# Two neighbouring PSUM banks for each tile of h, where any two were taken before, in a kernel of FFT, mixing, inverse FFT and a SoLU block

## The chip, the cores and the metric

The kernel runs on one core of a Trainium2 chip. The metric is the device time of one execution in microseconds (us); the figure of a kernel is the median of its runs. A change of under 0.5% can't be told from none here.

## The reference

```python
def _attn_ref(x, w_r, w_i, b_r, b_i):            # x: 8 x 3136 x 256
    X = np.fft.rfft(x, axis=1)
    Yr = X.real @ w_r - X.imag @ w_i + b_r
    Yi = X.real @ w_i + X.imag @ w_r + b_i
    Yr = np.sign(Yr) * np.maximum(np.abs(Yr) - 0.01, 0.0)      # Yi likewise
    return np.fft.irfft(Yr + 1j * Yi, n=3136, axis=1)

def _moe_ref(x, w_in, w_out, g_ln):              # x: 25088 tokens x 256
    h = x @ w_in                                 # 1024 wide
    e = np.exp(h - h.max(-1, keepdims=True))
    solu = h * e / (e.sum(-1, keepdims=True) + 1e-9)
    ln = (solu - solu.mean(-1)) / np.sqrt(solu.var(-1) + 1e-6) * g_ln
    return ln @ w_out
```

The output of the first function, seen as 25088 rows, is the input of the second. All data is f32 at the edges; inside, most products are made of f16 halves (a high and a low part).

## The kernel before

The FFT of length 3136 is done as 98 x 32 for each of eight batches b. In the names of the code: `fwd1` is the transform over 98 (its result goes to DRAM as `s1`), `fwd2` the one over 32 (`bin` in, `Xh` and `Xl` out), `mix` the product with w_r and w_i with the threshold (`yt`, `yc`, `y`, then `yh` and `yl`), `inv1` and `inv2` the way back (`zout` to DRAM as `s2`, `zt` in, `ring_hi` and `ring_lo` out). The ring holds the transformed rows with the 256 channels on the partitions, ready to be the stationary operand.

The second function takes tiles of 128 tokens, 196 in all. `moe_head` makes h = 128 x 1024 in PSUM: 12 matmuls of 512 columns (`win_hi`, `win_lo`, `win_low`), six for each half of h. h fills two banks, since a bank holds 512 f32 per partition. Three large instructions then read the whole of h: VectorE takes the maximum (`TENSOR_REDUCE sm<-banks`), ScalarE the exponential (`ACTIVATE u<-banks,sm,hsb`), VectorE the product (`SCALAR_TENSOR_TENSOR u<-banks,sm,u`). They are called the readers of h below. `moe_turn` splits u into halves (`lh` on ScalarE, `ll` on GpSimd) and transposes both by DMA into `th` and `tl`. `moe_tail` is the product with w_out: 16 matmuls with `th` and then 8 with `tl`, which go on adding up in the same half of one bank, that of the tile `po`; ScalarE reads it into `o` at the end.

All eight PSUM banks are one tensor, `banks` (class `Banks`). Four kinds of tiles live in it: `pf` and `pb` (the FFT of later batches and of batch 0), `ph` (h, two banks) and `po` (the tail), each with a limit on how many may be open (`BANKS`). Which bank a tile gets is decided by `Plan.order`.

`Plan` records all operations of the kernel, and `Plan.order` lists them: with estimated lengths it goes through the time of the five engines, and on each engine takes, among the operations that may start within `PATIENCE` ns of the first, the one with the lowest key. `KEYS` holds the numbers from which these keys are made: each h, tail, step of the FFT or piece of weight preparation gets a due place on the scale of token tiles. A bank is free in the plan when the last user of its tile is done. `issue` then gives the operations to the engines in the plan's order, and semaphores are set between instructions by a layer below, from the tensors and the parts of them that the instructions name. For h the named part is the slice that `Banks.place` returns:

```python
a, z = min(banks), max(banks)
return self.whole[:, a] if a == z else self.whole[:, a : z + 1 : z - a]
```

A pair of banks 3 and 6 is so a slice from 3 to 6 with step 3.

Of the kernel before, what the change touches and what calls it, by code (L numbers as in the profile page):

```python
# [39 lines left out]


KEYS = dict(
    front_b0=(-134.43, 2.81),
    w_in=(-129.4, -109.93, -44.57),
    w_out=(-102.26, -0.89),
    mix_w=30.03,
    front_a1=(-80.28, -2.98),
    front_a=((-15.77, 8.71), (-6.29, 0.76)),
    front_b=((-1.1, -4.17), (-1.83, 0.4)),
    inv2=-69.22,  # L50
    turn=2.98,
    tail=4.41,
)
BANKS = dict(pf=7, ph=8, po=8, pb=4)


def fft_constants():
# [78 lines left out]
class View:  # L136
# [5 lines left out]
    def __init__(self, tile, rows, cells, dtype, path=()):  # L142
        self.tile, self.rows, self.cells, self.dtype, self.path = tile, rows, cells, dtype, path
# [113 lines left out]
class Banks:  # L257


    def __init__(self, pool, n, **most):  # L260
        self.pool, self.kinds = pool, {name: Kind(m, self) for name, m in most.items()}
        self.n, self.whole, self.ordered = n, None, False
        self.free = [(0.0, i) for i in range(n)]

    def place(self, banks):
        if self.whole is None:
            self.whole = self.pool.tile([128, self.n, 512], F32, name="banks")
        a, z = min(banks), max(banks)
        return self.whole[:, a] if a == z else self.whole[:, a : z + 1 : z - a]

    def tile(self, name):
        t = Tile(self.pool, self.kinds[name], [128, 512], F32, dict(name=name, bufs=1))
# [8 lines left out]
class Slots:  # L281


    def __init__(self, pool, n, name, shape):
        self.pool, self.n, self.name, self.shape, self.ordered = pool, n, name, shape, True
        self.kind, self.whole = Kind(n, self), None
        self.free = [(0.0, i) for i in range(n)]

    def memory(self):
        if self.whole is None:  # L290
# [24 lines left out]
class Plan:  # L315
# [2 lines left out]


    ENGINES = ("gpsimd", "tensor", "vector", "scalar", "sync")  # L320
    PATIENCE = 150.0
    BACKLOG, AHEAD = 3200.0, 1500.0
    LEAVE = {2: 115.0, 4: 150.0, 8: 195.0}

# [102 lines left out]
    def order(self):  # L427
        ready = {e: [] for e in self.ENGINES}
        free = dict.fromkeys(self.ENGINES, 0.0)
        waits, bus, half, port = {}, 0.0, False, 0.0  # L430
        for op in self.ops:
            waits[op] = len(op.needs)
            for o in op.needs:
                o.next.append(op)
            if not op.needs:
                op.at = 0.0
                ready[op.engine].append(op)
        left = {t: len(t.users) for op in self.ops for t in op.tiles}

        turn, turns = {}, {}  # L440
        for t, op in sorted(((t, min(t.users, key=lambda op: op.seq)) for t in left), key=lambda x: (x[1].key, x[1].seq)):
            if t.kind.banks is None or t.kind.banks.ordered:
                turn[t] = turns.get(t.kind, 0)
                turns[t.kind] = turn[t] + 1
        done = []

        def may_start(op):
            at = max(free[op.engine], op.at, port if op.port else 0.0, bus - (self.AHEAD if op.early else self.BACKLOG) if op.moved else 0.0)
            taken = {}
            for t in op.tiles:  # L450
                if t.owner is None:
                    k = t.kind
                    n = len(k.placed) + taken.get(k, 0)
                    taken[k] = taken.get(k, 0) + 1
                    if turn.get(t, n) != n:
                        return np.inf
                    n -= k.bufs
                    if n >= 0:
                        at = max(at, k.freed[n] if n < len(k.freed) else np.inf)
                    if k.banks is not None:  # L460
                        n, spare = taken.get(k.banks, 0) + t.size, k.banks.free
                        taken[k.banks] = n
                        at = max(at, spare[n - 1][0] if n <= len(spare) else np.inf)
            return at

        while len(done) < len(self.ops):
            best = None
            for e in self.ENGINES:
                can = [(may_start(op), op) for op in ready[e]]
                if not can:  # L470
                    continue
                first = min(at for at, _ in can)
                if first == np.inf:
                    continue
                _, _, at, op = min((op.key, op.seq, at, op) for at, op in can if at <= first + self.PATIENCE)
                if best is None or at < best[0]:
                    best = at, op
            assert best is not None, "the plan is stuck"
            at, op = best
            e = op.engine  # L480
            ready[e].remove(op)
            if e == "tensor":
                if op.half != half:
                    at += 95.0 if op.half else self.LEAVE[half]
                half = op.half
            op.start = at
            op.end = free[e] = at + op.length
            if op.port:
                port = op.end
            if op.moved:  # L490
                bus = max(bus, op.end) + op.moved
                op.end = bus + 2000.0
            for t in op.tiles:
                if t.owner is None:
                    t.owner = op
                    t.kind.placed.append(t)
                    if t.kind.banks is not None:
                        t.banks = [t.kind.banks.free.pop(0)[1] for _ in range(t.size)]
                left[t] -= 1
                if not left[t]:  # L500
                    freed = max(o.end + self.SEEN[o.engine] for o in t.users)
                    insort(t.kind.freed, freed)
                    if t.kind.banks is not None:
                        for bank in t.banks:
                            insort(t.kind.banks.free, (freed, bank))
            for o in op.next:
                waits[o] -= 1
                if not waits[o]:
                    o.at = max(p.end + (0.0 if p.engine == o.engine == "tensor" else self.SEEN[p.engine]) for p in o.needs)
                    ready[o.engine].append(o)  # L510
            done.append(op)
        self.span = max(op.end for op in done)
        return sorted(done, key=lambda op: (op.start, op.seq))
# [22 lines left out]
def fft_mix_solu_kernel(ctx: ExitStack, tc, x, w_r, w_i, b_r, b_i, w_in, w_out, g_ln, fa, ff, iaf, fb, fs, gb, gs, ia, out):  # L536
# [17 lines left out]
    sp = Pool(ctx.enter_context(tc.tile_pool(name="sp", bufs=4)), 4)  # L554
    banks = Banks(ctx.enter_context(tc.tile_pool(name="ps", bufs=1, space=PSUM)), 8, **BANKS)

# [916 lines left out]
```

## Time and profile before

| | |
|---|---|
| median of 3 runs | 1878.6 us (1873.95 to 1882.69) |
| the profiled execution | 1879.95 us, of it 1878.2 us from the first to the last instruction (the span) |
| TensorE (PE) | 1568.8 us busy, 84% of the span |
| VectorE (DVE), ScalarE (ACT), GpSimd (POOL) | 1221.5, 1146.5 and 1173.5 us busy: 65%, 61% and 62% |
| mean granted clock of TensorE | 0.964 of the full 2.4 GHz |

PE is a busy matmul unit, PEld its weight loads. Since a helper of the kernel records every operation, all rows have one line (L425), and groups are told apart by the names of the tiles. "Idle before" a group is the time in which its engine stood idle just ahead of one of its instructions, with what ended that wait.

### The profile page before, as it was taken

The page shows a single profiled execution, that of the slowest core. Times are in us where ns is not written, and L with a number is a line of the kernel's source. Part 1 is how long each engine was busy: PE and PEld are TensorE (multiplying, and loading weights), DVE is VectorE, ACT ScalarE, POOL GpSimd, SP SyncE. Part 2 cuts the span into 40 slices and gives each one's busy share as a digit, 9 for nine tenths or more (in the row PEclk, how much of TensorE's full clock was granted, in tenths as well). Part 3 has the DMA queues.
Part 4 walks back from the last instruction along what each step waited for, and adds up shares of the span by engine and source line. Part 5 has one row for each costly group of instructions (what it writes and reads, how often), then busy time and mean ns, then how long its engine had stood idle before and what let it go on. Part 6 is the DMA issues. An engine that isn't in the chain of part 4 may idle for free. (4 is left out here: it accounts for less than half of the span.)

```text
span 1878.2 us, 41461 instructions
## 1 busy us (share of the span) xinstructions
PE 1568.8 (84%) x15471; PEld 1059.3 (56%) x15471; DVE 1221.5 (65%) x2496; ACT 1146.5 (61%) x2092; POOL 1173.5 (62%) x1701
## 2 busy tenths in 40 slices
PE   6977988878887888988986879887788888778888
PEld 3444665646555565665654556565555666455555
DVE  4996777556765676867774567666677666545543
ACT  4776766565656565666664567565566666456665
POOL 1646876656755676677664667666676666555565
PEclk7989999989999999999998999999999999999999
DMA  6895878546787766988676767777665955456655
GB/s 212 246 263 120 181 176 169 138 99 142 159 172 158 139 146 146 202 181 169 142 172 139 150 135 163 165 175 161 139 136 129 191 100 116 88 112 124 124 101 107
DMA packets 538815, 285.69 MB, mean 152 GB/s; under 512 B 428900, under 2 KB 507216, under 8 KB 538612
## 3 DMA queue, kind: packets, MB, share of 16 engines
q1 hardware_dynamic: 538164, 281.43, 68.7%
q8 instruction: 121, 1.98, 0.5%
q10 hardware_dynamic: 448, 1.61, 0.3%
q14 instruction: 82, 0.67, 0.1%
HBM read 103.10 MB, written 77.07 MB: 96 GB/s over the span
## 5 line engine op out<-in xcount | busy, mean ns | idle before, releaser
L425 POOL TENSOR_TENSOR ll<-u,lh 128x1024 f16<-128x1024 f32 x196 | 420.2, 2144 | 191.5 <-ACT lh L425 188.6
L425 DVE SCALAR_TENSOR_TENSOR u<-banks,sm,u 128x1024 f32<-128x1024 f32 x196 | 251.2, 1282 | 270.3 <-PE banks L425 139.2
L425 PE MATMUL banks<-wout,th 128*128 128x256 f16 x3136 | 384.9, 277 | 29.1 <-DVE u L425 19.7
L425 ACT ACTIVATE u<-banks,sm,hsb 128x1024 f32<-128x1024 f32 x192 | 231.2, 1204 | 226.7 <-PE banks L425 161.5
L425 PE MATMUL banks<-win_hi,ring_hi 128*128 128x512 f16 x768 | 296.6, 386 | 85.2 <-DVE u L425 44.6
L425 PEld LDWEIGHTS <-th 128*128 128x128 f16 x3136 | 308.3, 99 | 100.3 <-issue 44.4
L425 DVE TENSOR_REDUCE sm<-banks 128x1 f32<-128x1024 f32 x196 | 239.6, 1222 | 180.8 <-PE banks L425 174.2
L425 ACT CAST lh<-u 128x1024 f16<-128x1024 f32 x196 | 205.6, 1049 | 186.6 <-DVE u L425 119.1
L425 PE MATMUL banks<-win_low,ring_lo 128*128 128x512 f16 x768 | 296.7, 386 | 0.0
L425 PE MATMUL banks<-win_lo,ring_hi 128*128 128x512 f16 x768 | 296.6, 386 | 0.0
L425 PEld LDWEIGHTS <-ring_hi 128*128 128x128 f16 x1536 | 150.4, 99 | 248.5 <-issue 117.2
L425 PE MATMUL banks<-wout,tl 128*128 128x256 f16 x1568 | 206.6, 275 | 64.3 <-DVE sm L425 38.8
L425 ACT ACTIVATE junk<-u,sm 128x1024 bf16<-128x1024 f32 x196 | 226.0, 1153 | 5.2 <-DVE u L425 5.2
L425 PEld LDWEIGHTS <-tl 128*128 128x128 f16 x1568 | 153.4, 99 | 95.8 <-issue 74.2
L425 PE MATMUL banks<-w_hi,Xh 128*128 128x256 f16 (+1 forms) x584 | 168.9, 289 | 45.5 <-DVE u L425 19.6
L425 POOL TENSOR_SCALAR a<-sm 128x1 f32<-128x1 f32 x196 | 54.8, 279 | 202.6 <-ACT u L425 152.0
L425 POOL TENSOR_TENSOR y<-yt,yc 128x512 f32<-128x512 f32 (+1 forms) x104 | 134.2, 1291 | 70.8 <-DVE yc L425 53.1
L425 PE MATMUL banks<-w_hi,Xl 128*128 128x256 f16 (+1 forms) x584 | 168.9, 289 | 1.0 <-DVE Xl L425 1.0
L425 PE MATMUL banks<-w_lo,Xh 128*128 128x256 f16 (+1 forms) x584 | 168.8, 289 | 0.0
L425 PEld LDWEIGHTS <-Xh 128*128 128x128 f16 x1168 | 114.9, 100 | 89.6 <-issue 55.5
L425 POOL TENSOR_TENSOR yl<-y,yh 128x512 f16<-128x512 f32 x96 | 115.4, 1202 | 40.4 <-ACT yh L425 39.9
L425 ACT ACTIVATE o<-banks,r 128x256 f32<-128x256 f32 x196 | 92.8, 474 | 77.8 <-PE banks L425 42.9
(179 smaller groups left out, 2567.8 us busy)
## 6 DMA issues: line engine op xcount, KB each, us to landing
xt_all<-in_x_dram SPq DMA_DIRECT2D x56, 392.0 KB
zt<-s SPq DMA_DIRECT2D x56, 392.0 KB
s<-zout SPq DMA_DIRECT2D x42, 512.0 KB
xt_all<-in_x_dram SPq DMA_DIRECT2D x96, 192.0 KB
s<-av SPq DMA_DIRECT2D x96, 192.0 KB
bin<-s SPq DMA_DIRECT2D x72, 256.0 KB
out_dram<-o SPq DMA_DIRECT2D x128, 96.0 KB
out_dram<-o SPq DMA_DIRECT2D x136, 64.0 KB
```

What stands on the lines that cost most here:

```text
L425: getattr(engine, name)(*args, **kw)
```

## The change

`Banks.place` returns a slice of two banks that lie side by side. The list of free banks, kept in the order of time before, becomes one time of release per bank. A pair is taken where two neighbours are both free soonest; a single bank is taken, among those that are free, where it has the fewest free neighbours (`pick`), so that pairs of free banks are kept. `may_start` asks for a free neighbouring pair. The limits of the kinds become pf 8, ph 5, po 8, pb 5, `PATIENCE` goes from 150 to 84 ns, and the numbers of `KEYS` are others. No operation is added, removed or changed in size.

```diff
 KEYS = dict(
-    front_b0=(-134.43, 2.81),
-    w_in=(-129.4, -109.93, -44.57),
+    front_b0=(-144.94, 2.65),
+    w_in=(-135.14, -99.06, -27.81),
...
-BANKS = dict(pf=7, ph=8, po=8, pb=4)
+BANKS = dict(pf=8, ph=5, po=8, pb=5)
...
     def place(self, banks):
-        a, z = min(banks), max(banks)
-        return self.whole[:, a] if a == z else self.whole[:, a : z + 1 : z - a]
+        a, n = banks[0], len(banks)
+        return self.whole[:, a] if n == 1 else self.whole[:, a : a + n]
...
-    PATIENCE = 150.0
+    PATIENCE = 84.0
...
                     if k.banks is not None:
-                        n, spare = taken.get(k.banks, 0) + t.size, k.banks.free
+                        n, spare = taken.get(k.banks, 0) + 1, k.banks.free
                         taken[k.banks] = n
-                        at = max(at, spare[n - 1][0] if n <= len(spare) else np.inf)
+                        at = max(at, sorted(spare)[n - 1] if t.size == 1 else min(map(max, spare, spare[1:])))
             return at
+
+        def pick(free, size, at):
+            if size == 2:
+                a = min(range(len(free) - 1), key=lambda i: (max(free[i], free[i + 1]), i))
+                banks = [a, a + 1]
+            else:
+                beside = lambda i: sum(0 <= j < len(free) and free[j] <= at for j in (i - 1, i + 1))
+                banks = [min(range(len(free)), key=lambda i: (free[i] > at, beside(i), free[i], i))]
+            for i in banks:
+                free[i] = np.inf
+            return banks
...
-                        t.banks = [t.kind.banks.free.pop(0)[1] for _ in range(t.size)]
+                        t.banks = pick(t.kind.banks.free, t.size, at)
```

The first place is on TensorE, in the tail of one of the early token tiles, where the matmuls with `th` end and those with `tl` begin. A name in brackets is a semaphore that the row awaits: `DMAHW` those of DMAs, `DVE` that of VectorE. Before:

```order
L425 MATMUL banks<-wout,th 128x256
L425 LDWEIGHTS tl [waits DMAHW1_49]
L425 MATMUL banks<-wout,tl 128x256 [waits DVE_49]
L425 LDWEIGHTS tl
L425 MATMUL banks<-wout,tl 128x256
```

The same place of a tail in the changed kernel:

```order
L425 MATMUL banks<-wout,th 128x256
L425 LDWEIGHTS tl [waits DMAHW5_49]
L425 MATMUL banks<-wout,tl 128x256
L425 LDWEIGHTS tl
```

Before, 45 of the 196 tails have a matmul with `tl` that awaits VectorE (38) or ScalarE (7); in the changed kernel none has, and the weight loads of `tl` go on waiting for the DMA that brings it.

The second place is on TensorE at the first tile of h. `th,ones` and `tl,ones` are the column sums of w_out, for which these buffers are lent; `wpeak` and `wtop` belong to the scales of the weights, `iaf_s,zt` is the last step of the inverse FFT. Before:

```order
L425 MATMUL banks<-th,ones 128x256 [waits Pool_49]
L425 MATMUL banks<-th,ones 128x256
L425 MATMUL banks<-tl,ones 128x256 [waits Activation_49] x2
L425 MATMUL banks<-ident,wpeak 1x128 [waits DVE_49]
L425 MATMUL banks<-iaf_s,zt 128x98 [waits DMAHW4_49]
L425 MATMUL banks<-iaf_s,zt 128x98 x7
L425 MATMUL banks<-iaf_s,zt 128x98 [waits DMAHW5_49]
L425 MATMUL banks<-iaf_s,zt 128x98 x7
L425 MATMUL banks<-ident,top 1x128 [waits DVE_49]
L425 MATMUL banks<-wtop,ones 128x1 [waits DVE_49]
L425 LDWEIGHTS ring_hi [waits Activation_49]
L425 MATMUL banks<-win_hi,ring_hi 128x512
```

In the changed kernel:

```order
L425 MATMUL banks<-iaf_s,zt 128x98 [waits DMAHW2_49]
L425 MATMUL banks<-iaf_s,zt 128x98 x7
L425 LDWEIGHTS ring_hi [waits Activation_49]
L425 MATMUL banks<-win_hi,ring_hi 128x512 [waits DVE_49]
...
L425 MATMUL banks<-win_low,ring_lo 128x512
L425 MATMUL banks<-th,ones 128x256 [waits Pool_49]
L425 MATMUL banks<-th,ones 128x256
```

The first h has moved ahead of the column sums of w_out, which now stand inside it; it awaits the last scaling of w_in on VectorE instead.

## Rows read from the trace of the kernel before

**Rows 1.** The head of the page and its first part: busy time of each engine, its share of the span, and instructions.

```profile
span 1878.2 us, 41461 instructions
PE 1568.8 (84%) x15471; PEld 1059.3 (56%) x15471; DVE 1221.5 (65%) x2496; ACT 1146.5 (61%) x2092; POOL 1173.5 (62%) x1701
```

**Rows 2.** The view of who waited for whom, TensorE alone: us in total, number of waits, the longest.

```profile
PE banks L425 <- DVE u L425: 104.9, 83, 3.4
PE banks L425 <- DVE sm L425: 79.0, 69, 2.6
PE banks L425 <- ACT u L425: 70.2, 56, 3.4
PE banks L425 <- ACT bin L425: 15.4, 2, 9.7
PE banks L425 <- DMA xt_all<-in_x_dram: 9.7, 5, 2.7
```

**Rows 3.** Groups of instructions on TensorE: count | busy us, mean ns of one | idle us before them and what ended it.

```profile
L425 PE MATMUL banks<-wout,tl 128*128 128x256 f16 x1568 | 206.6, 275 | 64.3 <-DVE sm L425 38.8 <-ACT u L425 10.3 <-DVE u L425 10.2
L425 PE MATMUL banks<-wout,th 128*128 128x256 f16 x3136 | 384.9, 277 | 29.1 <-DVE u L425 19.7 <-DVE sm L425 4.8 <-DMA xt_all<-in_x_dram 2.7
L425 PE MATMUL banks<-win_hi,ring_hi 128*128 128x512 f16 x768 | 296.6, 386 | 85.2 <-DVE u L425 44.6 <-ACT u L425 32.5 <-DVE sm L425 7.4
L425 PE MATMUL banks<-w_hi,Xh 128*128 128x256 f16 (+1 forms) x584 | 168.9, 289 | 45.5 <-DVE u L425 19.6 <-DVE sm L425 12.0 <-ACT u L425 9.3
L425 PE MATMUL banks<-ia_s,zt 98*128 98x98 f16 x1344 | 72.1, 207 | 18.0 <-DVE sm L425 10.4 <-ACT u L425 3.8 <-DVE u L425 2.2
```

**Rows 4.** The timeline from 1000 to 1024 us, the rows of PE, DVE and ACT around two tails and the tile of h between them: start us, duration us, engine, operation, count, idle time before and what ended it.

```profile
1000.25 0.63 PE L425 MATMUL banks<-win_low,ring_lo 128*128 128x512 f16 x1
...
1001.10 1.28 DVE L425 SCALAR_TENSOR_TENSOR u<-banks,sm,u 128x1024 f32<-128x1024 f32 x1 [3.96 <-PE banks L425]
...
1002.44 3.56 PE L425 MATMUL banks<-wout,th 128*128 128x256 f16 x16 [1.56 <-DVE u L425]
...
1006.11 1.22 DVE L425 TENSOR_REDUCE sm<-banks 128x1 f32<-128x1024 f32 x1 [3.72 <-PE banks L425]
...
1007.39 1.03 PE L425 MATMUL banks<-wout,tl 128*128 128x256 f16 x8 [1.39 <-DVE sm L425]
...
1009.75 1.21 ACT L425 ACTIVATE u<-banks,sm,hsb 128x1024 f32<-128x1024 f32 x1 [5.10 <-PE banks L425]
...
1011.51 1.28 DVE L425 SCALAR_TENSOR_TENSOR u<-banks,sm,u 128x1024 f32<-128x1024 f32 x1 [3.49 <-POOL a L425]
...
1012.86 1.91 PE L425 MATMUL banks<-wout,th 128*128 128x256 f16 x16 [1.85 <-DVE u L425]
```

**Rows 5.** Who waited for whom, all engines, the three large waits of the readers of h for TensorE.

```profile
DVE sm L425 <- PE banks L425: 174.2, 119, 4.2
ACT u L425 <- PE banks L425: 162.2, 75, 6.0
...
DVE u L425 <- PE banks L425: 139.2, 52, 5.9
```

**Rows 6.** The core's row: span and mean granted clock.

```profile
core 0: 1878.2 us, clock 0.964
```

**Rows 7.** Busy us of each engine (and instructions) in two stretches, the start up to 188 us and the rest; then the granted clock of TensorE (1.00 is 2.4 GHz, 0.50 is 1.2 GHz), the share of the DMA engines, GB/s.

```profile
0.00:188.00 188.00, 145.10 (x1291) 80.79 (x1292) 137.69 (x302) 121.42 (x230) 88.03 (x99) 0.88 0.74 210
188.00:1878.00 1690.00, 1423.73 (x14182) 978.49 (x14180) 1083.80 (x2196) 1025.08 (x1863) 1085.48 (x1602) 0.97 0.69 146
```

**Rows 8.** The same view as rows 7, three stretches of 6.8 us that follow each other.

```profile
985.40:992.20 6.80, 6.63 (x132) 4.68 (x132) 5.41 (x9) 4.78 (x9) 4.56 (x6) 1.00 0.87 158
992.20:999.00 6.80, 4.82 (x36) 3.32 (x34) 3.76 (x10) 5.29 (x9) 3.44 (x6) 1.00 0.81 196
999.00:1005.80 6.80, 5.24 (x21) 2.93 (x20) 1.29 (x2) 2.19 (x3) 3.53 (x5) 0.50 0.82 195
```

More of the change, by code (lines that the diff above doesn't have):

```diff
@@ L42 @@
 KEYS = dict(
-    front_b0=(-134.43, 2.81),
-    w_in=(-129.4, -109.93, -44.57),
[L45 to L52, printed above, removed]
+    front_b0=(-144.94, 2.65),
+    w_in=(-135.14, -99.06, -27.81),
+    w_out=(-82.19, -2.79),
+    mix_w=110.96,
+    front_a1=(-62.31, 0.45),
+    front_a=((-28.87, -0.64), (-10.37, -3.83)),
+    front_b=((1.32, -0.24), (0.25, 1.29)),
+    inv2=-54.08,
+    turn=3.86,
+    tail=5.93,
 )
-BANKS = dict(pf=7, ph=8, po=8, pb=4)
+BANKS = dict(pf=8, ph=5, po=8, pb=5)
 def fft_constants():
@@ L262, in __init__ @@
         self.n, self.whole, self.ordered = n, None, False
-        self.free = [(0.0, i) for i in range(n)]
+        self.free = [0.0] * n
     def place(self, banks):
@@ L286, in __init__ @@
         self.kind, self.whole = Kind(n, self), None
-        self.free = [(0.0, i) for i in range(n)]
+        self.free = [0.0] * n
     def memory(self):
@@ L504, in order @@
                         for bank in t.banks:
-                            insort(t.kind.banks.free, (freed, bank))
+                            t.kind.banks.free[bank] = freed
             for o in op.next:
```

## The prediction

> **What bounds the kernel now.** I read the busy times first. TensorE is busy for 1568.8 of 1878.2 us and no other engine for more than 65% of the span [rows 1], so TensorE is the engine to follow, and 1878.2 - 1568.8 = 309.4 us is what it idles. The view of its waits says what ends this idle time: readers of h on VectorE and ScalarE, with 104.9 + 79.0 + 70.2 = 254.1 us in 208 waits [rows 2]. All other waits together are 309.4 - 254.1 = 55.3 us. So the kernel is bound by TensorE plus waits for the readers of h.
>
> The next question is whether these waits are owed. The groups answer it [rows 3]. The matmuls with `tl` idle 64.3 us, of which 38.8 + 10.3 + 10.2 = 59.3 us end with a reader of h. But they go on adding to the bank that the matmuls with `th` have opened just before: nobody else can hold that bank, and `tl` itself comes by DMA. Nothing that they need is made by a reader of h. The timeline shows one such case [rows 4]: a tail adds up with `th` from 1002.44; the maximum of another tile of h, due since long, has stood 3.72 us for TensorE and starts when the `th` part is over, at 1006.11; the `tl` part of the tail then stands 1.39 us for that maximum. The two block each other in turn though they touch different tiles. The slice of `Banks.place` explains it: a pair a and z, named as one slice with a step, covers the banks between them if whoever sets the semaphores goes by its ends, and a tail that lies in such a bank is kept apart from every reader of that h. In the built program of before, counted from each instruction's bank offset and the semaphore count that it awaits, this is what stands there: 258 of TensorE's waits name an instruction that reads or writes other banks only, yet each within the ends of a pair, 249 of VectorE's and 201 of ScalarE's (its waits for itself left out). In that of the changed kernel, counted alike, the three engines have none.
>
> **What the change does, part by part.**
>
> *Waits of TensorE for readers of h.* The change takes away those for a bank in between, and leaves those for a bank that h really held. How many of the 254.1 us are of the first kind? The lower bound is the 59.3 us of `tl`, which can't be anything else; the upper bound is all. To choose, I take the `tl` row as a rate: 59.3 / 196 tails = 0.30 us for each time that TensorE turns to a bank in use beside an open h. The other groups turn to a bank at least as often: 2 x 196 times for h, 196 times for `th`. At that rate they would wait 118 and 59 us; they wait 84.5 and 24.5 us for readers of h [rows 3]. Nothing is left over that would need a true wait as its cause, so I let all 254.1 us go.
>
> *What is late next.* TensorE then meets waits that were hidden behind these: for the halves `Xh`, `yh`, `th`, for DMAs, and for banks that h holds in earnest. The trace shows 55.3 us of waits with other causes. I let them nearly double, by 51 us, since everything else gets over a tenth less time to be ready. That leaves TensorE idle for 55 + 51 = 106 us. Bounds: nothing comes back, or half of the 254.1, 127 us, does. Net gain of these two terms: 254.1 - 51 = 203 us.
>
> *Waits of VectorE and ScalarE for TensorE.* The readers of h stand 174.2 + 139.2 + 162.2 = 475.6 us for TensorE [rows 5], partly for their own h, partly for a bank in between. What goes here is not added to the sum: both engines are under 66% busy [rows 1], and they are on the path only through what TensorE waits for. It makes the chain of a tile of h shorter, from 6.7 us in the example (the maximum begins at 1006.11, the product ends at 1012.79 [rows 4]), and so works against the 51 us.
>
> *The clock.* The mean granted clock is 0.964 [rows 6], that is (1 - 0.964) x 1878.2 = 67.6 us at full speed lost; the start has (1 - 0.88) x 188 = 22.6 us of it [rows 7], the rest 45.0 us. In that rest TensorE is busy 1423.73 / 1690 = 84% of the time, so the low clock costs 0.84 x 45 = 38 us there. The rows tie it to idle time [rows 8]: full clock over 985.4 to 992.2 with 6.63 of 6.8 us busy, 4.82 busy in the next 6.8 us, and the half clock, 1.2 GHz, in the 6.8 us after that; the same 16 matmuls take 3.56 us there and 1.91 us at the next tail [rows 4]. With a third of the idle time left I count on half of the 38 us, 19 us. Bounds: 0 and 38.
>
> *The start.* In the first 188 us TensorE idles 188 - 145.1 = 42.9 us [rows 7], of it 15.4 us for `bin` and 9.7 us for input DMAs [rows 2]. The new keys let the first h go ahead of w_out's column sums, but it now needs w_in's scaling done earlier on VectorE. Gain and loss come out of the same work on VectorE (137.69 of 188 us busy); I take 0, and 15 us either way as bounds, the size of the wait for `bin`.
>
> *The rest.* Counts and sizes of instructions are unchanged: 0. A reader of two neighbouring banks has as many elements as one of two apart, and 46 of the 196 pairs of before are neighbours already (counted in the built program); its 1.22, 1.21 and 1.28 us [rows 4] are taken as they are. The transfers issued by SP move with their tiles' keys; the DMA engines are 69% busy after the start [rows 7] and would be near 0.69 x 1690 / 1468 = 79%: this is in the 51 us.
>
> *Sum.* 1878.2 - 203 - 19 = 1656.2 us of span. The profiled execution took 1879.95 us, 1.75 more than its span, and was 1.35 us above the median of the runs; 1656.2 + 1.75 - 1.35 = 1656.6, so **1657 us**. TensorE would be about (1568.8 - 19) / 1656 = 94% busy.
>
> **The rivals.**
>
> *Other engines take over.* At 1470 us for the part after 188 us, VectorE and GpSimd would be 1084 / 1470 = 74% busy, in chains that hand a tile on five times. If their queues give back half of the removed waits, the time is 1878.6 - 127 = 1752 us. For it: three engines of nearly equal load. Against it: the chain of h gets shorter too. 0.18.
>
> *The clock comes back fully.* If what idle time is left is too scattered to lower the clock, the whole 38 us return: 1657 - 19 = 1638 us, and with nothing of the waits coming back 1638 - 51 = 1587 us. For it: the stretches of rows 8. Against it: one wait of 2 us sufficed there. 0.12. By the Trainium skill ("TensorE: Matmul & The Clock Gate", Part 1) half speed is the default state, and activity releases it; rows 8 agree in their direction, and by that rule alone the clock's term would be 38 us.
>
> *The waits are owed after all.* Eight banks are few: an h keeps two for 6.7 us, about as long as TensorE has for a tile (1568.8 / 196 = 8.0 us). If TensorE's waits are for want of banks, and not for their order, they come back under other names, and the time stays at 1879. Against it: the `tl` row. 0.06. The Trainium skill ("Perfetto Trace Analysis", Optimization Strategy) says that the same gap repeated on the engine that should be saturated can mean too little PSUM; by that reading neighbouring pairs free nothing, and the sum would be 1879; the `tl` matmuls, which ask for no new bank, speak against it.
>
> *Pairs are hard to find.* Two banks side by side are both free less often than any two, and a single tile between splits a run of free ones. If every h and every tail waits the mean of a wait for the product today, 104.9 / 83 = 1.26 us, for that reason, 392 x 1.26 = 494 us come in and the time is 1879 - 254 + 494 = 2119 us. It decides from 254 / 392 = 0.65 us for each on. For it: the limit of ph falls to 5 and `PATIENCE` to 84. Against it: the plan sees this shortage and sets other work ahead, which it could not do for waits that it knew nothing of. 0.05.
>
> **How the numbers follow.** The forecast has 0.59 (about 1600 to 1710 us), the rivals 0.18, 0.12, 0.06 and 0.05. The range reaches down to the fuller return of the clock and up over the case of other engines: 1590 to 1760 us; it leaves out the last two rivals and the low end of the clock's. A difference of 0.5%, 9 us, is about what can be told here. Faster by more than that: 0.59 + 0.18 + 0.12 and a part of the third rival, 0.91; within it 0.04; slower 0.05.
>
> **What would show it.** In the profile of the changed kernel: no idle time ended by a reader of h ahead of `tl` (right if under 3 us; 59.3 us now); TensorE's waits for readers of h under 100 us (a sum near 254 would make the third rival right, above it the fourth); TensorE over 90% busy with its own busy time 1530 to 1570 us; the readers' waits for TensorE well under 475 us; a clock of 0.975 to 0.98 of the full one. Waits for `th`, `yh`, `Xh` or a DMA above 150 us would mean the first rival. The prediction fails if the semaphores of before come from true uses of a bank, since then the 254 us stay.

## The result, and the profile after

| | before | changed |
|---|---|---|
| median | 1879.53 us (4 runs, 1873.95 to 1882.69) | 1546.18 us (4 runs, 1541.35 to 1554.62) |
| ratio | | 0.8234 (95% interval 0.8191 to 0.8277) |
| span of the profiled execution | 1878.2 us | 1539.6 us |

Of the kernel before there is one run more here than in the table ahead of the prediction. The kernel got faster by 333 us. The forecast was 1657 us with a range of 1590 to 1760; the result lies below that range. So the sign was right and the size too small by 111 us: a third of the gain was not in the sum.

The head of the page of the changed kernel and its busy times, which answer to [rows 1]:

```profile
span 1539.6 us, 41444 instructions
PE 1498.2 (97%) x15471; PEld 1041.7 (68%) x15471; DVE 1211.9 (79%) x2496; ACT 1139.0 (74%) x2092; POOL 1184.8 (77%) x1701
```

TensorE's idle time fell from 309.4 to 1539.6 - 1498.2 = 41.4 us, by 268 us. Its busy time fell too, by 70.6 us, though every matmul is still there (x15471). The two add up to the whole 338.6 us of span.

TensorE's longest waits in the changed kernel, as in [rows 2], us in total, number, the longest:

```profile
PE banks L425 <- DMA zt<-s2f: 5.8, 1, 5.8
PE banks L425 <- ACT bin L425: 5.7, 1, 5.7
PE banks L425 <- DMA zt<-s: 3.9, 3, 2.4
PE banks L425 <- DMA xt_all<-in_x_dram: 3.7, 1, 3.7
PE banks L425 <- DVE u L425: 2.5, 1, 2.5
```

Of 254.1 us behind readers of h one wait of 2.5 us is left (it stands in the start, at 144 us, ahead of a matmul `iaf_s,zt`), and nothing of that size has come in its place: the longest entry is a single wait for a DMA. The groups of [rows 3] in the changed kernel:

```profile
L425 PE MATMUL banks<-wout,th 128*128 128x256 f16 x3136 | 374.7, 273 | 1.3 <-DMA th<-lh 1.3
...
L425 PE MATMUL banks<-win_hi,ring_hi 128*128 128x512 f16 x768 | 292.3, 381 | 0.4 <-DVE v L425 0.4
...
L425 PE MATMUL banks<-wout,tl 128*128 128x256 f16 x1568 | 203.4, 273 | 0.0
...
L425 PE MATMUL banks<-w_hi,Xh 128*128 128x256 f16 (+1 forms) x584 | 165.4, 283 | 3.6 <-ACT Xh L425 2.0 <-DVE yt L425 1.1 <-ACT zout L425 0.2
```

The matmuls with `tl` stand 0.0 us, against 64.3. The timeline shows a tail and a maximum of h side by side, which in [rows 4] shut each other out:

```profile
1003.96 1.91 PE L425 MATMUL banks<-wout,th 128*128 128x256 f16 x16
...
1004.16 1.22 DVE L425 TENSOR_REDUCE sm<-banks 128x1 f32<-128x1024 f32 x1 [0.96 <-PE banks L425]
...
1005.70 1.04 PE L425 MATMUL banks<-wout,tl 128*128 128x256 f16 x8
```

The maximum begins 0.2 us after the tail's first matmul and is over before `tl`, which follows without a wait.

The readers' two longest waits in the view of all engines, as in [rows 5]:

```profile
DVE u L425 <- ACT u L425: 101.5, 120, 2.3
DVE sm L425 <- PE banks L425: 96.1, 104, 3.1
```

The two stretches, with the same columns as [rows 7]:

```profile
0.00:188.00 188.00, 157.37 (x1274) 89.28 (x1275) 135.58 (x308) 124.05 (x235) 98.02 (x120) 0.87 0.73 211
188.00:1539.60 1351.60, 1340.82 (x14199) 952.45 (x14197) 1076.29 (x2189) 1014.92 (x1858) 1086.80 (x1582) 1.00 0.87 182
```

The core's row, as [rows 6]:

```profile
core 0: 1539.6 us, clock 0.984
```

The product (`DVE u`) no longer stands for TensorE at all but mostly for the exponential that it needs, and the maximum's wait for TensorE is down from 174.2 to 96.1 us. From 188 us on TensorE is busy 1340.82 of 1351.6 us, at a granted clock that rounds to 1.00.

### The profile page after: what moved, and what is told of

It is laid out like the page before. It is cut to its first block, busy times and chain, and to the rows that moved or that the text cites. A ratio compares the mean times of both kernels' runs of the same rounds, so it can differ in the third digit from the quotient of the medians.

```text
span 1539.6 us, 41444 instructions
## 1 busy us (share of the span) xinstructions
PE 1498.2 (97%) x15471; PEld 1041.7 (68%) x15471; DVE 1211.9 (79%) x2496; ACT 1139.0 (74%) x2092; POOL 1184.8 (77%) x1701
## 4 chain that ended last, share of the span: by engine, by line
PE 88%; DMA 4%; DVE 2%; ACT 2%; POOL 2%; issue 1%; SPq 1%; POOLq 0%; ACTq 0%; DVEq 0%
PE banks L425 88%; DMA zt<-s 1%; DMA xt_all<-in_x_dram 1%; SPq L425 1%; ACT u L425 1%; DMA th<-lh 1%; DVE sm L425 0%; DMA zt<-s2f 0%; DMA xt_all<-s1f 0%; POOL y L425 0%; POOL yl L425 0%; DVE peaks L425 0%; DVE u L425 0%; POOL xt_all L569 0%; DMA s1f<-tl 0%
## 5 line engine op out<-in xcount | busy, mean ns | idle before, releaser
L425 PE MATMUL banks<-wout,th 128*128 128x256 f16 x3136 | 374.7, 273 | 1.3 <-DMA th<-lh 1.3
L425 PEld LDWEIGHTS <-th 128*128 128x128 f16 x3136 | 302.9, 98 | 57.9 <-issue 8.7
L425 DVE TENSOR_REDUCE sm<-banks 128x1 f32<-128x1024 f32 x196 | 239.2, 1220 | 96.8 <-PE banks L425 96.1
L425 PE MATMUL banks<-win_hi,ring_hi 128*128 128x512 f16 x768 | 292.3, 381 | 0.4 <-DVE v L425 0.4
L425 PE MATMUL banks<-win_lo,ring_hi 128*128 128x512 f16 x768 | 292.1, 380 | 0.0
L425 PE MATMUL banks<-win_low,ring_lo 128*128 128x512 f16 x768 | 291.9, 380 | 0.0
L425 PE MATMUL banks<-w_hi,Xh 128*128 128x256 f16 (+1 forms) x584 | 165.4, 283 | 3.6 <-ACT Xh L425 2.0
L425 PE MATMUL banks<-w_hi,Xl 128*128 128x256 f16 (+1 forms) x584 | 165.0, 283 | 0.6 <-DVE Xl L425 0.5
L425 PE MATMUL banks<-w_lo,Xh 128*128 128x256 f16 (+1 forms) x584 | 165.2, 283 | 0.0
L425 POOL TENSOR_SCALAR a<-a,hsb 128x1 f32<-128x1 f32 x384 | 126.0, 328 | 16.4
L425 PEld LDWEIGHTS <-ring_lo 128*128 128x128 f16 x768 | 75.3, 98 | 91.3 <-issue 1.0
```

What stands on the lines that cost most here:

```text
L425: getattr(engine, name)(*args, **kw)
```

## The experiments

Theory S: the slice with a step alone makes the waits, since the layer that sets semaphores takes it for all banks between its ends. Theory K: a good part of the gain is the new keys and the order. In all runs with any two banks or renamed banks "waits for a bank in between" are counted in the built program, as in the prediction. All times are medians of four runs, with the ratio to seven runs of the kernel before taken beside them: 1878.24 us for the old order with neighbours, the renamed banks, the exchange of 3 and 4 and the old keys, 1876.87 us for the other four.

### The order of before, neighbouring banks

The keys, limits, patience and the order of every engine are those of before, row for row. When the plan is finished, a search hands out the bank numbers anew, such that each h has two neighbours and no tile has to wait for a bank longer than the plan had it wait.

```diff
-        a, z = min(banks), max(banks)
-        return self.whole[:, a] if a == z else self.whole[:, a : z + 1 : z - a]
+        a, n = banks[0], len(banks)
+        return self.whole[:, a] if n == 1 else self.whole[:, a : a + n]
...
         self.span = max(op.end for op in done)
+        self.neighbours(done)
...
```

`neighbours` is the search; it gives every tile new `banks` from its start and end in the plan.

> The order of before on every engine, instruction by instruction, with its keys; only the bank numbers are given anew after the plan is made, so that each h has two neighbours. The built program then has no wait of TensorE, VectorE or ScalarE for a bank in between (258, 249 and 201 in before). Theory S (the stepped slice alone makes the waits, and keys and order give next to nothing): the 254 us of idle time go, and with them about 208 x 0.165 = 34 us of running empty at each stop and up to 38 us of low clock: 1879 - 254 - 34 - 38 = 1553 us, say 1540 to 1590. Theory K (keys and order give a good part of the 333 us): 1640 us or more.

Measured: 1548.43 us, ratio to before 0.8254 (0.8228 to 0.828). The whole gain is there with the old order, inside the range of theory S. The busy times of this run:

```profile
PE 1493.6 (97%) x15471; PEld 1040.2 (67%) x15471; DVE 1220.5 (79%) x2496; ACT 1137.5 (74%) x2092; POOL 1177.2 (76%) x1701
```

TensorE's three longest waits in it:

```profile
PE banks L425 <- ACT bin L425: 10.2, 2, 5.8
PE banks L425 <- DVE Xl L425: 5.1, 5, 2.7
PE banks L425 <- ACT zout L425: 4.2, 1, 4.2
```

Its groups of matmuls with `th` and with `tl`:

```profile
L425 PE MATMUL banks<-wout,th 128*128 128x256 f16 x3136 | 374.8, 273 | 2.2 <-DMA th<-lh 2.1
...
L425 PE MATMUL banks<-wout,tl 128*128 128x256 f16 x1568 | 203.4, 273 | 1.1 <-DMA tl<-ll 1.1
```

TensorE idles 1542.1 - 1493.6 = 48.5 us, 261 us less than in the same order with any two banks. Theory K falls.

### The order of the change, banks renamed

```diff
-        a, n = banks[0], len(banks)
-        return self.whole[:, a] if n == 1 else self.whole[:, a : a + n]
+        banks = [3 * i % 8 for i in banks]
+        a, z = min(banks), max(banks)
+        return self.whole[:, a] if a == z else self.whole[:, a : z + 1 : z - a]
```

> The order of the changed kernel on every engine, with its keys and its plan of the banks, but bank i is named 3i mod 8, so that every pair that was neighbours is 3 or 5 apart. The built program has 349 waits of TensorE, 310 of VectorE and 267 of ScalarE for banks in between. Theory S: by the 333 us for 258 such waits, 349 give 450 us: 1546 + 450 = about 1990 us, at least 1850 us. Theory K: at most 1720 us, as the better keys are all there. A third theory, that the chip reads two neighbouring banks faster than two apart, would show in the readers of h, 1.22, 1.21 and 1.28 us, which S expects to be unchanged.

Measured: 1937.38 us, ratio to before 1.033 (1.0284 to 1.0377). With nothing changed but the names of the banks, 391 us come in. TensorE's longest waits (the helper that records operations stands on line 426 in this run, the next two and the split one):

```profile
PE banks L426 <- DVE u L426: 128.5, 100, 4.0
PE banks L426 <- ACT u L426: 98.1, 92, 3.0
PE banks L426 <- DVE sm L426: 81.6, 80, 2.8
```

The groups of the maximum and of the matmuls with `tl`, columns as in [rows 3]:

```profile
L426 DVE TENSOR_REDUCE sm<-banks 128x1 f32<-128x1024 f32 x196 | 239.6, 1222 | 194.1 <-PE banks L426 173.7 <-ACT u L426 16.1 <-ACT junk L426 1.6
...
L426 PE MATMUL banks<-wout,tl 128*128 128x256 f16 x1568 | 205.5, 274 | 65.8 <-ACT u L426 22.8 <-DVE sm L426 18.7 <-DVE u L426 17.5
```

308.2 us behind readers of h, and `tl` waits again. The maximum takes 1222 ns over pairs 3 or 5 apart and 1220 ns (239.2 us for 196) over neighbours in the changed kernel, so at these distances it takes no longer. The waits cost 391 / 349 = 1.12 us each, less than in before (333 / 258 = 1.29), so the expected 1990 us was too high, its bound of 1850 right.

### Banks 3 and 4, and banks 0 and 7, exchanged

The same edit with `banks = [{3: 4, 4: 3}.get(i, i) for i in banks]`, and with `{0: 7, 7: 0}`.

> The changed kernel with the names of banks 3 and 4 exchanged: pairs 2-3 and 4-5 become 2-4 and 3-5 (49 of 196 tiles of h), one bank between; all others stay neighbours. The built program has 55 waits of TensorE for a bank in between. Theory S with a cost in proportion: 55 / 258 x 333 = 71 us more than the changed kernel, 1617 us; if the waits hinder each other (a blocks b and b blocks a), less than in proportion, 1570 to 1600 us. Theory K: 1546 us, no change.

> The changed kernel's order with the names of banks 0 and 7 exchanged: pairs 0-1 and 6-7 (65 of 196 tiles of h) become 1-7 and 0-6, five banks between; the other 131 stay neighbours. The built program has 168 waits of TensorE for a bank in between. Theory S (the stepped slice makes the waits): more than with banks 3 and 4 exchanged (55 such waits, 1585 us). At that run's 0.72 us for each, 168 give 121 us, 1667 us; at the 1.29 us of before, 217 us, 1763 us. Between these two, so 1660 to 1770 us.

Measured: 1585.28 us (0.8455, 0.8429 to 0.8482) and 1811.39 us (0.9667, 0.962 to 0.9713). The first is inside what S expected for waits that hinder each other, the second above the range of S, 1660 to 1770 us. TensorE's waits for readers of h with banks 3 and 4 exchanged:

```profile
PE banks L426 <- DVE u L426: 19.9, 22, 2.5
PE banks L426 <- DVE sm L426: 8.7, 11, 1.3
...
PE banks L426 <- ACT u L426: 4.4, 6, 2.1
```

The same with banks 0 and 7 exchanged:

```profile
PE banks L426 <- DVE u L426: 87.6, 59, 2.5
PE banks L426 <- ACT u L426: 71.6, 54, 3.1
PE banks L426 <- DVE sm L426: 56.9, 48, 2.5
```

49 tiles that cover one bank more cost 39 us, 0.80 us a tile; 65 tiles that cover five banks more cost 265 us, 4.1 us a tile. The cost goes with the number of banks covered (5.1 times as much a tile for 5 times the banks), and by the count of waits in the program (55 and 168) it was wrongly scaled: 0.71 and 1.58 us each. Two runs alone would not make that a rule, but the renamed run has the same order too: counted in its built program, its 196 pairs cover 482 banks more, and 391 / 482 = 0.81 us. In the kernel before, in another order, it is 333 us for 391 banks, 0.85 us. That waits hinder each other is not needed to explain the first run.

### Banks apart, readers split

The renaming by 3i mod 8, and each reader of h as two instructions of one bank each, with two small sums; `exp` and the product in the same way.

```diff
-        nc.vector.tensor_reduce(m, p, AX.XY, ALU.max, negate=True)
-        nc.vector.tensor_scalar(m, m, down, None, ALU.mult)
...
+        for h, part in enumerate((m, m1)):
+            nc.vector.tensor_reduce(part, p[:, h], AX.X, ALU.max, negate=True)
+        nc.vector.tensor_scalar(m, m, m1, down, ALU.min, ALU.mult)
...
```

> Pairs 3 or 5 apart by renaming, as in the second run, but each of the three readers of h is split into two instructions, one for each bank, so that no slice has a step (two maxima with their minimum of the negated values, two exponentials, two products, and two small sums). Theory S: the built program has no wait for a bank in between, so the time stays near the changed kernel's, plus what the extra instructions cost: VectorE gets about 0.6 us more for each of 196 tiles, 118 us, and would be near 85% busy: 1550 to 1650 us. If banks apart cost something on the chip itself, or if it is not the slice that makes the waits: 1900 us or more, as in the second run (1937 us).

Measured: 1609.64 us (0.8581, 0.856 to 0.8601), inside the range of S. The busy times:

```profile
PE 1524.6 (95%) x15471; PEld 1055.9 (66%) x15471; DVE 1360.4 (84%) x3280; ACT 1202.5 (75%) x2484; POOL 1215.3 (75%) x1897
```

The matmuls with `tl`:

```profile
L426 PE MATMUL banks<-wout,tl 128*128 128x256 f16 x1568 | 206.1, 275 | 0.0
```

TensorE's waits for readers of h, all that are left:

```profile
PE banks L426 <- DVE u L426: 1.8, 3, 1.2
...
PE banks L426 <- DVE sm L426: 1.4, 2, 1.2
```

With banks as far apart as in the run of 1937 us, but no slice with a step, TensorE's waits for readers of h are down from 308.2 to 3.2 us. It is the slice. Neighbouring banks are the cheaper cure: VectorE carries 148 us more here than in the changed kernel (1211.9 us).

### Old keys in the new plan, new keys with any two banks

The changed kernel with `KEYS`, `BANKS` and `PATIENCE` of before, and the kernel before with those of the changed one.

> The changed kernel with the keys, the limits of the kinds and the patience of before: the plan knows of neighbouring pairs, but its numbers were not made for them. Theory S: as e1, 1540 to 1600 us. Theory K: 1640 us or more. If pairs are hard to find with the old limits (ph 8), TensorE waits for the readers of its own bank, over 50 us of them, and the time is above that of e1 by as much.

> The kernel before with the keys, limits and patience of the changed one, any two banks for h. The built program has 288 waits of TensorE for a bank in between. Theory S: 1546 + 333 x 288 / 258 = 1918 us, 1840 to 1940 us. If the new keys were worth something by themselves: under 1840 us.

Measured: 1558.85 us (0.8307, 0.8289 to 0.8325) and 1932.26 us (1.0303, 1.028 to 1.0325). Both are inside the ranges of S. In the new plan the new keys, limits and patience are worth 13 us; but the old keys in the old order, with neighbours given afterwards, took 1548.43 us, which can't be told from the changed kernel. With any two banks the new set costs 55 us, and TensorE's waits there say where:

```profile
PE banks L425 <- DVE u L425: 135.6, 98, 2.9
PE banks L425 <- ACT u L425: 83.7, 76, 3.0
PE banks L425 <- DVE sm L425: 78.6, 69, 2.0
```

That is 297.9 us behind readers of h, 44 us more than before, from 288 waits for a bank in between instead of 258. So most of what the new keys cost there is more of the same waits. The prediction counted the keys at 0.

### One tile of h at a time

```diff
-BANKS = dict(pf=8, ph=5, po=8, pb=5)
+BANKS = dict(pf=8, ph=1, po=8, pb=5)
```

> The changed kernel with at most one tile of h open at a time (limit of ph 1 instead of 5), with neighbouring banks. Here TensorE's waits for the readers of h are owed. Theory S: they stand ahead of the first matmul of h alone, none ahead of the matmuls with tl (59.3 us in before); so waits that are owed look other than those of before. Time: 196 tiles by 2.6 us of matmuls and 5.0 to 6.7 us of readers, after a start of 135 us: 1625 to 1960 us. The rival that the waits of before were owed, for want of banks, expects the pattern of before, with waits ahead of tl too.

Measured: 1734.05 us (0.9237, 0.9212 to 0.9261). The time is in the range, but the waits do not stand where S put them, as three groups on TensorE show:

```profile
L425 PE MATMUL banks<-wout,th 128*128 128x256 f16 x3136 | 388.7, 279 | 116.4 <-DMA th<-lh 112.4 <-ACT u L425 2.0 <-ACT o L425 1.2
L425 PE MATMUL banks<-win_hi,ring_hi 128*128 128x512 f16 x768 | 297.2, 387 | 6.3 <-DVE u L425 6.0
...
L425 PE MATMUL banks<-wout,tl 128*128 128x256 f16 x1568 | 204.3, 273 | 3.2 <-DMA tl<-ll 3.2
```

This shortage, which the plan knows of, hardly appears as waits for readers of h: TensorE stands ahead of `th`, for a transpose. A likely reading, not tried by itself, is that the plan puts other work where h would have to wait, and then runs out of it. Neither S's guess (ahead of h) nor the pattern of before shows. That speaks against the third rival too: this want of banks looks other than [rows 2, 3].

## Why the prediction was right in its sign and wrong in its size

**What bounds the kernel, and the false waits: right.** TensorE bound it, and the waits for readers of h were not owed. That they come from the slice is shown, by the same order with neighbours (1548 us), the same order renamed (1937 us) and the split readers (1610 us). "Let all 254.1 us go" was right to 2.5 us, though its argument did not reach so far: the rate from the `tl` row was held against 59.3 + 84.5 + 24.5 = 168.3 us, and for the other 85.8 us, ahead of `w_hi`, `ia_s` and others, the prediction gave none. For that part the choice was lucky.

**"What is late next", the 51 us: wrong, and the step that failed first.** The prediction let the waits with other causes nearly double, because everything else would get over a tenth less time. Instead they fell from 55.3 us to about 39. There was no row behind the doubling. The run with the order of before shows that it is not the new keys that prevent it: there too TensorE idles 48.5 us in all, and `th` and `tl` together wait 3.2 us for their DMAs. The likely reason is that the plan's order had been made without knowledge of the false waits and had the data ready for a TensorE that doesn't stop. Idle time taken away, net: 203 us forecast, 268 measured.

**"The clock", 19 us: too small.** The granted clock rose from 0.964 to 0.984, the loss at full speed fell from 67.6 to (1 - 0.984) x 1539.6 = 24.6 us. What such a loss costs can be read from repeated runs of one kernel: the changed kernel took 1539.6, 1541.8, 1547.0 and 1552.8 us of span at clocks 0.984, 0.983, 0.980 and 0.976, that is losses of 24.6, 26.2, 30.9 and 37.3 us: 1.03 us of span for each us. Seven runs of the kernel before, 1869.4 us at 0.970 to 1877.7 us at 0.966, give 0.94 (0.82 in the other seven); the other eight kernels, four runs each, scatter from 0.5 to 1.3, most of them with clocks that differ by little more than the last digit given. So the clock is worth about 0.9 x 67.6 - 1.03 x 24.6 = 35 us, an estimate, near the upper bound of 38 rather than the middle. The two stretches say the same: from 188 us on the granted clock rounds to 1.00, and the start alone has (1 - 0.87) x 188 = 24.4 us of the 24.6 us lost. So the 45.0 us of loss in the rest are almost all gone, where the forecast counted on half.

**The term that was missing: running empty.** 70.6 us of busy time went and the clock explains about half. The timeline of the changed kernel shows two matmuls of h in a row:

```profile
1006.58 0.38 PE L425 MATMUL banks<-win_hi,ring_hi 128*128 128x512 f16 x1
...
1006.79 0.38 PE L425 MATMUL banks<-win_lo,ring_hi 128*128 128x512 f16 x1
```

Each lasts 0.38 us in the profile, but over the 12 matmuls of this h, from 1006.58 to 1008.95, the starts lie 0.215 us apart on average; at a stop, the remaining 0.165 us are counted as busy, though nothing is started in them. The 16 matmuls with `th` shown further up give the same: they fill 1.91 us at a mean of 0.273 us, so their starts lie (1.91 - 0.273) / 15 = 0.109 us apart, and 0.164 us remain. 208 waits x 0.165 = 34 us, and 35 + 34 = 69 of the 70.6 us. The idle time before a wait is thus less than what the wait costs. The expectation of the first experiment had this term and came to 1553 us against 1548. No run changes this term alone, but the ten profiles of this case bear it out: a fit of TensorE's busy time gives 1473 us, plus 0.77 us for each us of clock loss, plus 0.20 us for each of TensorE's waits (243 before, 25 in the changed kernel, 305 with renamed banks), to within 5 us; with the loss alone it misses by up to 23 us. Loss and waits rise together from run to run, so how the 70.6 us are shared between the two is known only roughly.

**"The start", 0:** TensorE idles 30.6 us there instead of 42.9, 12 us better; in the order of before with neighbours it is 188 - 153.53 = 34.5 us. That is within the bounds of 15. The row of the latter, as in [rows 7]:

```profile
0.00:188.00 188.00, 153.53 (x1376) 88.11 (x1377) 147.12 (x320) 130.82 (x248) 99.27 (x117) 0.89 0.78 220
```

**The rivals.** Other engines didn't take over, though VectorE is at 79%. The clock's rival, with a chance of 0.12, was right that the low clock goes almost wholly after the start; its low end, 1587 us with nothing of the waits coming back, was nearest to the result, and the range left it out. "Owed after all" and "pairs are hard to find" are both excluded: in the very order of before a search found neighbours for every h without one late tile, and the kernel took 1548 us.

**The signs.** The waits ahead of `tl` and for the readers came out as named. TensorE's own busy time, 1498.2 us, is below the 1530 to 1570 us expected, and the clock, 0.984, above 0.975 to 0.98: the same two terms, running empty and the clock, again.

So, of the 1656.2 - 1539.6 = 116.6 us of span between forecast and result, 65 are waits that didn't come back or went besides, and by the estimates above 16 are the clock and 34 the running empty.

## What to carry to other kernels

Where an accumulation that is under way waits for the reader of another tile, look at how that reader names its operand: two banks given as one slice with a step held up everything between its ends. The waits taken out here, of a kernel whose order was planned without them, gave back all of their time, plus what the engine ran empty and most of the low clock, so those belong in the sum. Keys tuned for one placement of tiles can lose in another: the same set was worth 13 us in one and cost 55 in the other.

## What the runs showed of the hardware that was not expected

- The spread between runs of one kernel goes with the clock: 1539.6 to 1552.8 us in step with 0.984 to 0.976. Only one of the four has a profile, so what set the clock apart is not shown.
- Reading 128 x 1024 f32 from two banks takes VectorE's maximum the same time at every distance tried: 1220 ns for neighbours in the changed kernel (1223 ns with one pair at a time), 1222 ns for banks 3 or 5 apart, 1223 ns in the run with pairs 6 apart among them.
- With TensorE busy 99% of the time after the start (1340.82 of 1351.6 us) the DMA engines carried a share of 0.87 there, up from 0.69, and in that stretch TensorE waited for DMAs only five times, 5.2 us in all.
